# Pairwise softmax on VectorE, and b2 added by DMA, in a fused attention and MLP kernel on one Trainium2 core

## The chip, the cores and the metric

The kernel runs on one core of a Trainium2 chip. The metric is device time in microseconds (us); lower is better. A profile's span, from its first instruction to its last, is some 1.8 us shorter than the run's time.

PE is TensorE (PEld its weight loads), DVE is VectorE, ACT is ScalarE, POOL is GpSimd, and SP is the engine whose queue issues nearly all the DMAs. A "q" behind a name (SPq, POOLq) means the engine's instruction queue.

## The reference

```python
h  = x + attention(layernorm(x), wqkv) @ wo     # 32 heads of 18, window of 8 positions, 2 apart
h2 = h + gelu(layernorm(layernorm(h)) @ w1 + b1) @ w2 + b2
# x: 1 x 2048 x 576, w1: 576 x 4608, w2: 4608 x 576, all bf16
```

Each query attends to eight keys: its own position and those 2, 4, ... 14 before it, with softmax over the eight.

## The kernel before

The 2048 rows are 16 tiles of 128 rows, worked in eight pairs. After a prologue (LN1 and the QKV products) the program for PE is, for each pair: the first MLP matmul of this pair (four "visits" of two or three PSUM banks each, result `pm`), the output projection of the next pair (`pw`), and the second MLP matmul of this pair (result `po`, two tiles). The other engines work ahead: for the next pair, `h` and LN2; for the pair after that, attention. The last two pairs use a Strassen-like scheme with seven products, whose sums of w2 blocks VectorE prepares earlier.

The softmax of one tile, by VectorE with one exp on ScalarE:

```python
def att_qk_b(j, skip=0):
    att_qk_add(j, ((0, 0, 9), (0, 0, 4), (0, 0, 2), (0, 0, 1))[skip:])
    logits = sb.tile([P, W, H], F32, tag="logits", name="logits", bufs=2)
    nc.vector.tensor_tensor(out=logits[:], in0=prod[:, :, 0:H], in1=prod[:, :, 8 * H:9 * H], op=ALU.add)
    # ... causal mask of row 0
    nc.vector.tensor_reduce(out=mx[:], in_=logits[:].rearrange("p w h -> p h w"), axis=AX.X, op=ALU.max)
    nc.vector.tensor_tensor(out=logits[:], in0=logits[:], in1=mx[:].unsqueeze(1).to_broadcast([P, W, H]),
                            op=ALU.subtract)
```

A tile's keys and values are used by its own attention and then replaced by a copy shifted by one row, which comes back from DRAM. That is the "halo": `halo(j, 1)` fetches keys and `halo(j, 2)` values, both through the SP queue. And a transposed tile (LN2's output as `hnT`, attention's output o as `oT`) is written to DRAM (`td`) and read back by a transposing DMA, also through the SP queue, which stands still until the write has landed:

```python
def dma_transpose(dst, src):
    td = dma_out(src)
    nc.sync.dma_start_transpose(out=dst, in_=td[:])
```

LN2 of a pair ended with b2 added on VectorE, so that `x_all` holds the residual for the output addition:

```python
def add_b2(j):
    nc.vector.tensor_tensor(out=x_all[:, j, :], in0=h_of.pop(j)[:], in1=b2_bc[:], op=ALU.add)
```

The kernel keeps a PSUM bank's first half visit and second half visit on PE apart: a no-op on GpSimd, the "marker", waits for the first, and PE waits for it before the second.

## Time and profile before

| | before |
|---|---|
| median | 371.94 us (371.36, 371.82, 372.05, and one run of 542.28) |
| span, granted clock | 369.8 us, 0.998 |
| PE, VectorE, ScalarE busy | 98%, 81%, 65% |

The first three runs of the kernel before, without the 371.82, have the median of 372.05 us that the prediction starts from.

The page's table of engines of the kernel before (busy us, share of the span, instructions):

```profile
PE 363.2 (98%) x4944; PEld 299.4 (81%) x4944; DVE 299.3 (81%) x452; ACT 239.1 (65%) x519; POOL 25.2 (7%) x35
```

The waits of PE in the kernel before (who waited for whom: us in total, times, longest):

```profile
PE busy L661 <- DVE prod L654: 1.5, 1, 1.5
PE pm L209 <- ACT hT L490: 0.5, 1, 0.5
...
```

The chain of waits of the kernel before, one pair of it (start, us, what):

```profile
108.72 17.79 PE pm L209 x324
126.52 2.21 PE pw L209 x36
128.72 17.75 PE po L505 x144
146.47 17.79 PE pm L209 x324
```

The chain is followed back from the last instruction. From the second pair on it is PE and nothing else until the last addition, 37.75 us for each pair. VectorE's 81% is therefore an average over work that PE hides.

### The profile page before, as it was taken

The numbers are of one execution on the slowest core, as the hardware profiler recorded it, in microseconds if no ns is written. First come the engines' busy times: TensorE is split into PE (matmuls) and PEld (weight loads), VectorE is DVE, ScalarE is ACT, GpSimd is POOL, SyncE is SP. The second block draws the span as 40 slices with busy tenths as digits, with TensorE's granted clock in tenths as the row PEclk, the third lists the DMA queues.
The fourth block names the chain that finished last, engine by engine and source line by source line (L and its number), as shares of the span: only waits on it lengthen the run. The fifth ranks groups of instructions, "written<-read, shape, count | busy, mean of one in ns | idle before, by whom it ended". The sixth has DMA issues, their size and how long they took to land.

```text
span 369.8 us, 11478 instructions
## 1 busy us (share of the span) xinstructions
PE 363.2 (98%) x4944; PEld 299.4 (81%) x4944; DVE 299.3 (81%) x452; ACT 239.1 (65%) x519; POOL 25.2 (7%) x35
## 2 busy tenths in 40 slices
PE   7999999999999999999999999999999999999996
PEld 4789877888788877887788778877887788778874
DVE  6899999999999798979897989889898986532332
ACT  2688756797738793679366936693669456735630
POOL 2322004000300010001000100000000000000000
PEclk9999999999999999999999999999999999999999
DMA  8979798956445104710431043104320411030000
GB/s 242 318 198 282 190 204 235 331 178 76 141 107 166 35 15 111 275 35 2 110 97 37 2 106 102 37 2 105 86 52 3 105 52 39 0 89 18 4 0 32
DMA packets 57265, 38.96 MB, mean 105 GB/s; under 512 B 31344, under 2 KB 55536, under 8 KB 57216
## 3 DMA queue, kind: packets, MB, share of 16 engines
q1 hardware_dynamic: 57056, 38.18, 38.6%
q8 instruction: 38, 0.62, 0.7%
q10 hardware_dynamic: 160, 0.07, 0.1%
q14 instruction: 11, 0.09, 0.1%
HBM read 19.92 MB, written 12.42 MB: 87 GB/s over the span
## 4 chain that ended last, share of the span: by engine, by line
PE 84%; DVE 11%; ACT 2%; POOL 1%; issue 1%; POOLq 0%; DVEq 0%
PE pm L209 37%; PE po L505 29%; PE po L576 8%; PE pw L209 5%; PE pq L209 4%; DVE ln_stats L145 2%; DVE prod L323 2%; DVE prod L362 1%; DVE prod L317 1%; PE busy L661 1%; DVE prod L366 1%; POOL ln_rstd L156 1%; ACT hT L490 1%; DVE ln_mv L146 1%; ACT L463 0%
## 5 line engine op out<-in xcount | busy, mean ns | idle before, releaser
L209 PE MATMUL pm<-hnT,w_sb 64*128 64x256 bf16 x2304 | 143.0, 269 | 0.5 <-ACT hT L490 0.5
L490 ACT ACTIVATE hT<-pm,b_sb 128x256 bf16<-128x256 f32 (+1 forms) x288 | 108.5, 498 | 48.4 <-PE pm L209 48.4
L209 PEld LDWEIGHTS <-w_sb 64*128 64x128 bf16 x2304 | 112.5, 94 | 15.0 <-issue 2.3
L505 PEld LDWEIGHTS <-hT 128*128 128x128 bf16 x864 | 84.0, 98 | 22.6 <-issue 1.7
L505 PE MATMUL po<-w2a_sb,hT 128*128 128x288 bf16 x672 | 84.5, 286 | 0.0
L209 PE MATMUL pq<-wq_sb,xnT 64*128 64x288 bf16 x768 | 54.0, 283 | 0.4 <-ACT xnT L255 0.2
L209 PEld LDWEIGHTS <-xnT 64*128 64x128 bf16 x864 | 44.1, 94 | 9.1 <-issue 0.4
L323 DVE TENSOR_TENSOR prod<-prod 128x2304 bf16<-128x2304 bf16 (+1 forms) x64 | 44.2, 691 | 2.1
L362 DVE TENSOR_TENSOR prod<-kv_ring,a 128x4608 bf16<-128x4608 bf16 x16 | 40.9, 2558 | 0.6
L317 DVE TENSOR_TENSOR prod<-kv_ring,q_all 128x4608 bf16<-128x4608 bf16 x16 | 40.8, 2552 | 0.2
L209 PE MATMUL pm<-hnT,w1h_sb 64*128 64x256 bf16 x288 | 39.4, 269 | 0.0
L366 DVE TENSOR_TENSOR prod<-prod 128x2304 bf16<-128x2304 bf16 (+1 forms) x32 | 33.9, 1058 | 1.1
L345 ACT ACTIVATE logits<-logits 128x256 f32<-128x256 f32 x16 | 6.7, 417 | 38.1 <-DVE logits L334 38.1
L423 POOL TENSOR_TENSOR ln_rstd<-ln_var,mhalf 128x1 f32<-128x1 f32 x14 | 11.3, 810 | 249.8 <-ACT ln_var L422 249.6
L505 PE MATMUL po<-w2b_sb,hT 128*128 128x288 bf16 x192 | 25.5, 286 | 0.0
L294 ACT CAST kv_ring<-pq 128x576 bf16<-128x576 f32 x32 | 19.4, 641 | 8.4 <-PE pq L209 8.4
L407 DVE TENSOR_TENSOR h<-pw,x_all 128x576 f32<-128x576 f32 x16 | 11.4, 751 | 14.0 <-PE pw L209 14.0
L209 PE MATMUL pw<-wo_sb,oT 64*128 64x288 bf16 x256 | 19.5, 283 | 0.2
L463 ACT ACT_TABLE_LOAD x14 | 18.0, 1283 | 0.2
L552 DVE TENSOR_TENSOR prod<-hT 128x512 f16<-128x512 f16 (+1 forms) x8 | 3.6, 455 | 17.6 <-ACT hT L490 17.6
L209 PEld LDWEIGHTS <-oT 64*128 64x128 bf16 x288 | 13.9, 94 | 4.3 <-POOLq L219 0.8
L345 ACT ACT_TABLE_LOAD x13 | 16.7, 1283 | 0.2
(98 smaller groups left out, 340.4 us busy)
## 6 DMA issues: line engine op xcount, KB each, us to landing
w_sb<-in_B_w_dram SPq DMA_DIRECT2D x6, 768.0 KB, 6.0
kv_ring<-kv_dram SPq DMA_DIRECT2D x28, 144.0 KB, 2.8
w2a_sb<-in_B_w_dram SPq DMA_DIRECT2D x4, 1008.0 KB, 6.5
kv_dram<-kv_ring SPq DMA_DIRECT2D x13, 288.0 KB, 3.5
out_dram<-o_sb SPq DMA_DIRECT2D x15, 144.0 KB, 2.9
td<-q_all SPq DMA_DIRECT2D x14, 144.0 KB, 2.4
td<-hn SPq DMA_DIRECT2D x14, 144.0 KB, 1.8
wq_sb<-in_A_wqkv_dram SPq DMA_DIRECT2D x3, 576.0 KB, 5.9
```

The source lines that it names most:

```text
L209: last = nc.tensor.matmul(duo["g"][r ^ swap][i], lhsT=lhsT, rhs=rhs, start=(swap == 0 and i == 0 and kt == 0), stop=(swap == 1 and kt == K ...
L294: pace[0] = nc.scalar.copy(out=dst.rearrange("p (d g h) -> p g d h", g=2, h=H // 2), in_=ps[:, :, 0:HALF].rearrange("p g (h d) -> p g d h" ...
L317: nc.vector.tensor_tensor(out=prod[:], in0=k_ring[j % 2], in1=q_all[:, j, :].unsqueeze(1) .to_broadcast([P, W, D]), op=ALU.mult)
L323: nc.vector.tensor_tensor(out=prod[:, :, o * H:o * H + n], in0=prod[:, :, a * H:a * H + n], in1=prod[:, :, c * H:c * H + n], op=ALU.add)
L345: nc.scalar.activation(out=logits[:], in_=logits[:], func=ACT.Exp, scale=SCALE)
L362: nc.vector.tensor_tensor(out=prod[:].rearrange("p w (d h) -> p w d h", h=H), in0=v_ring[j % 2].rearrange("p w (d h) -> p w d h", h=H), in ...
L366: nc.vector.tensor_tensor(out=prod[:, 0:n, :], in0=prod[:, 0:n, :], in1=prod[:, n:2 * n, :], op=ALU.add)
L407: nc.vector.tensor_tensor(out=h[:].rearrange("p (g c) -> p g c", g=2), in0=pw[:, :, 0:HALF], in1=x_all[:, j, :].rearrange("p (g c) -> p g ...
L463: nc.scalar.activation(out=warm[:], in_=mhalf[:], func=ACT.Gelu_apprx_tanh)
L490: pace[0] = nc.scalar.activation(out=hT[us[i // GF]][:, GF * r + i % GF, 0:N], in_=ps[:, r, i * N:(i + 1) * N], func=ACT.Gelu_apprx_tanh, ...
L505: nc.tensor.matmul(banks[half], lhsT=hT[f // (2 * GF)][:, f % (2 * GF), i * P:(i + 1) * P], rhs=w2_rows(f)[:, half * HALF:(half + 1) * HAL ...
L576: nc.tensor.matmul(bank, lhsT=l, rhs=r, start=(start and m == 0), stop=(m == NM - 1), skip_group_check=True)
```

## The change

Its intent is to relieve VectorE. From the fifth pair on, both tiles of a pair share one max, subtract, exp, sum, reciprocal and multiply; the fourth pair shares them too, in another order. Each addition of b2 becomes two DMAs: b2 is copied into `x_all` through the SP queue, and `h` is added to it by an accumulating DMA from GpSimd, made to wait for both LN2 transposes of the pair. The first and the last pair keep VectorE. One o of the third pair is sent and read back in two steps. The core of the diff:

```diff
+    def att_max(js):
+        n, sl = len(js), sides(js)
+        nc.vector.tensor_reduce(out=peak[:, sl], in_=logits[:, sl].rearrange("p i w h -> p i h w"), axis=AX.X, op=ALU.max)
+        nc.vector.tensor_tensor(out=logits[:, sl], in0=logits[:, sl],
+                                in1=peak[:, sl].unsqueeze(2).to_broadcast([P, n, W, H]), op=ALU.subtract)
+    def att_qk_pair(e, f):
+        for i, j in enumerate((e, f)):
+            att_qk_a(j)
+            halo(j, 1)
+            att_qk_b(j, i)
+        att_max([e, f])
+    def put_b2(j):
+        nc.sync.dma_start(out=x_all[:, j, :], in_=b2_bc[:])
+    def accumulate_h(j):
+        ins = nc.gpsimd.dma_start(out=x_all[:, j, :], in_=h_of.pop(j)[:], accum_op=ALU.add).ins
+        tc.add_manual_dep(ins, read[0].name, sync_dep, reason="behind the transposes of LN2")
 ... 
             elif c is not None:                       # all pairs but the first and last
-                m1[0].append(c_(pv_t, d))
-                if e is not None:
-                    m1[3] = m1.get(3, []) + [c_(att_qk, e)] + [c_(w2_sums, *m) for m in T_SUMS.get(k, ())]
-                    ia[0] = [c_(exps, e)]
-                ia[0] = ia.get(0, []) + [c_(wo_visit, (c, "B"), (d, "C")), c_(ln2_pair, c, d, e)]
 ... (k == 1, in which the fourth pair's attention is worked out, has lines of its own)
+                elif e is not None:
+                    m1[1] = [c_(att_qk_pair, e, f)]
+                    m1[3] = [c_(w2_sums, *m) for m in T_SUMS.get(k, ())]
+                    ia[0] = [c_(exps, e, f), wo, c_(ln2_pair, c, d, (e, f)), c_(dma_tr_o, e)]
                 ib[0] = [c_(finish_out, g[0])]
                 if e is not None:
-                    ia[2] = [c_(pv_sum, e), c_(dma_tr_o, e)]
-                    ib[2] = [c_(att_qk, f)] + ([c_(halos, 7)] if k == 1 else [])
-                    ib[32] = [c_(exps, f)]
+                    ib[2] = [c_(pv_sum, f), c_(dma_tr_o, f)]
```

`m1[n]` is work queued before visit n of the first MLP matmul, `ia[n]` and `ib[n]` work queued at step n of the second one's two tiles. So, from the fifth pair on, the attention of a pair's two tiles, which was spread over the whole period, is now back to back: both logit passes, then the w2 sums, and only then `h` (inside `ln2_pair`).

More of the change, by code (lines that the diff above doesn't have):

```diff
@@ L82 @@
     prod = wpool.tile([P, W, D], BF16, name="prod")
+    logits = wpool.tile([P, 2, W, H], F32, name="logits")
+    probs = wpool.tile([P, 2, W, H], BF16, name="probs")
+    peak = wpool.tile([P, 2, H], F32, name="peak")
+    den = wpool.tile([P, 2, H], F32, name="den")
     qp_cm = tc.tile_pool(name="qkvw", bufs=1)
@@ L140, in ln_stats @@
         n = len(srcs)
-        stats = sb.tile([P, n, 2, nc.vector.BN_STATS_DIM], F32, tag=f"{tag}_stats", name=f"{tag}_stats", bufs=bufs)
-        mv = sb.tile([P, n, nc.vector.BN_AGGR_DIM], F32, tag=f"{tag}_mv", name=f"{tag}_mv", bufs=bufs)
+        pool = qp if tag.startswith("ln1") else sb
+        stats = pool.tile([P, n, 2, nc.vector.BN_STATS_DIM], F32, tag=f"{tag}_stats", name=f"{tag}_stats", bufs=bufs)
+        mv = pool.tile([P, n, nc.vector.BN_AGGR_DIM], F32, tag=f"{tag}_mv", name=f"{tag}_mv", bufs=bufs)
         for i, src in enumerate(srcs):
@@ L306, in tr_b1, with sides @@
         nc.scalar.copy(out=b1_sb[:], in_=pt)
-    e_of = {}
+    side = {}
+    def sides(js):
+        i = side[js[0]]
+        return slice(i, i + len(js))
     def halo(j, t):
@@ L324, in att_qk_add, with att_qk_b, att_qk_rest, att_qk @@
                                     in1=prod[:, :, c * H:c * H + n], op=ALU.add)
-    def att_qk_b(j, skip=0):
+    def att_qk_b(j, i, skip=0):
+        side[j] = i
         att_qk_add(j, ((0, 0, 9), (0, 0, 4), (0, 0, 2), (0, 0, 1))[skip:])
-        logits = sb.tile([P, W, H], F32, tag="logits", name="logits", bufs=2)
-        nc.vector.tensor_tensor(out=logits[:], in0=prod[:, :, 0:H], in1=prod[:, :, 8 * H:9 * H], op=ALU.add)
+        nc.vector.tensor_tensor(out=logits[:, i], in0=prod[:, :, 0:H], in1=prod[:, :, 8 * H:9 * H], op=ALU.add)
         if j // 2 + 1 < W:
-            nc.vector.memset(logits[0:1, j // 2 + 1:W, :], -1e9)
-        mx = sb.tile([P, H], F32, tag="mx", name="mx")
-        nc.vector.tensor_reduce(out=mx[:], in_=logits[:].rearrange("p w h -> p h w"), axis=AX.X, op=ALU.max)
-        nc.vector.tensor_tensor(out=logits[:], in0=logits[:], in1=mx[:].unsqueeze(1).to_broadcast([P, W, H]),
-                                op=ALU.subtract)
-        e_of[j] = logits
-    def att_qk(j):
+            nc.vector.memset(logits[0:1, i, j // 2 + 1:W, :], -1e9)
+    def att_max(js):
[3 more added lines that the diff above has]
+                                in1=peak[:, sl].unsqueeze(2).to_broadcast([P, n, W, H]), op=ALU.subtract)
+    def att_qk_rest(j, i, skip=0):
+        att_qk_b(j, i, skip)
+        att_max([j])
+    def att_qk(j, i):
         att_qk_a(j)
         halo(j, 1)
-        att_qk_b(j)
-    def att_exp(j):
-        logits = e_of[j]
-        nc.scalar.activation(out=logits[:], in_=logits[:], func=ACT.Exp, scale=SCALE)
+        att_qk_rest(j, i)
+    def att_qk_pair(e, f):
[4 more added lines that the diff above has]
+        att_max([e, f])
+    def att_exp(*js):
+        sl = sides(js)
+        nc.scalar.activation(out=logits[:, sl], in_=logits[:, sl], func=ACT.Exp, scale=SCALE)
     def att_pv(j):
@@ L349, in att_pv, with att_den @@
         att_pv_sum(j)
-    def att_den(j):
-        e = e_of.pop(j)
-        den = sb.tile([P, H], F32, tag="den", name="den")
-        nc.vector.tensor_reduce(out=den[:], in_=e[:].rearrange("p w h -> p h w"), axis=AX.X, op=ALU.add)
-        nc.vector.reciprocal(out=den[:], in_=den[:])
-        a = sb.tile([P, W, H], BF16, tag="a", name="a")
-        nc.vector.tensor_tensor(out=a[:], in0=e[:], in1=den[:].unsqueeze(1).to_broadcast([P, W, H]), op=ALU.mult)
-        e_of[j] = a
+    def att_den(*js):
+        n, sl = len(js), sides(js)
+        nc.vector.tensor_reduce(out=den[:, sl], in_=logits[:, sl].rearrange("p i w h -> p i h w"), axis=AX.X, op=ALU.add)
+        nc.vector.reciprocal(out=den[:, sl], in_=den[:, sl])
+        nc.vector.tensor_tensor(out=probs[:, sl], in0=logits[:, sl],
+                                in1=den[:, sl].unsqueeze(2).to_broadcast([P, n, W, H]), op=ALU.mult)
     def att_pv_sum(j):
-        a = e_of.pop(j)
+        a = probs[:, side.pop(j)]
         nc.vector.tensor_tensor(out=prod[:].rearrange("p w (d h) -> p w d h", h=H),
                                 in0=v_ring[j % 2].rearrange("p w (d h) -> p w d h", h=H),
-                                in1=a[:].unsqueeze(2).to_broadcast([P, W, Dh, H]), op=ALU.mult)
+                                in1=a.unsqueeze(2).to_broadcast([P, W, Dh, H]), op=ALU.mult)
         for n in (4, 2):
@@ L386, in dma_tr_o, with send_o, read_o @@
         dma_transpose(new_oT(j)[:], q_all[:, j, :])
-    pw_of = {}
+    def send_o(j):
+        o_sent[j] = dma_out(q_all[:, j, :])
+    def read_o(j):
+        nc.sync.dma_start_transpose(out=new_oT(j)[:], in_=o_sent.pop(j)[:])
+    pw_of, o_sent = {}, {}
     def wo_duo(j, tag):
@@ L430, in ln2_send @@
         hn[j] = dma_out(y[:])
+    read = [None]
     def ln2_in(j):
-        nc.sync.dma_start_transpose(out=hnT_slot(j), in_=hn.pop(j)[:])
+        read[0] = nc.sync.dma_start_transpose(out=hnT_slot(j), in_=hn.pop(j)[:]).ins
     def add_b2(j):
         nc.vector.tensor_tensor(out=x_all[:, j, :], in0=h_of.pop(j)[:], in1=b2_bc[:], op=ALU.add)
+    def put_b2(j):
[3 more added lines that the diff above has]
+        tc.add_manual_dep(ins, read[0].name, sync_dep, reason="behind the transposes of LN2")
     def ln2_rstd(j):
@@ L722, in pv_t, with ln2_pair @@
             dma_tr_o(j)
-        def ln2_pair(c, d, e, b2=True):
+        def ln2_pair(c, d, js=()):
+            last = c == GROUPS[-1][0]
             for j in (c, d):
@@ L728, in ln2_pair @@
             for j in (c, d):
-                if b2:
-                    add_b2(j)
+                (add_b2 if last else put_b2)(j)
+            if js:
+                att_den(*js)
+                att_pv_sum(js[0])
+            for j in (c, d):
                 ln2_send(j)
+            if len(js) == 2:
+                halo(js[0], 2)
             for j in (c, d):
                 ln2_in(j)
-            if e is not None:
-                att_den(e)
+            if not last:
+                for j in (c, d):
+                    accumulate_h(j)
+            if len(js) == 1:
+                halo(js[0], 2)
         loads = {v: [c_(load_w1, c)] for c, v in enumerate((3, 4, 9, 14, 16, 18))}
@@ L747 @@
             6: [c_(ln1_rstd, 10), c_(ln1_act, 8, 2), c_(halo, A[0], 1)],
-            7: [c_(att_qk_b, A[0]), c_(ln1_bias, 10), c_(ln1_act, 8, 3), c_(in_x, 0), c_(out_x, 1)],
-            8: [c_(att_qk_a, A[1]), c_(att_qk_b, A[1]), c_(ln1_act, 9, 0)],
+            7: [c_(att_qk_rest, A[0], 0), c_(ln1_bias, 10), c_(ln1_act, 8, 3), c_(in_x, 0), c_(out_x, 1)],
+            8: [c_(att_qk_a, A[1]), c_(att_qk_rest, A[1], 1), c_(ln1_act, 9, 0)],
             9: [c_(halo, A[1], 1), c_(in_x, 1)],
@@ L760 @@
             19: [c_(ln2, A[1])],
-            20: [c_(ln2_rstd, A[1]), c_(add_b2, A[1]), c_(ln2_bias, A[1]), c_(att_qk_b, A[2], 1)],
+            20: [c_(ln2_rstd, A[1]), c_(add_b2, A[1]), c_(ln2_bias, A[1]), c_(att_qk_rest, A[2], 0, 1)],
         }
@@ L817, in halos, with exps @@
                 store_halo(pending_halo.pop(0))
-        def exps(j):
-            att_exp(j)
+        def exps(*js):
+            att_exp(*js)
             gelu_table()
@@ L836 @@
             if k == 0:
-                m1[0] += [c_(halos, 1), c_(att_qk_a, d), c_(att_qk_b, d), c_(halo, d, 1)]
+                m1[0] += [c_(halos, 1), c_(att_qk_a, d), c_(att_qk_rest, d, 1), c_(halo, d, 1)]
                 mid[0] = [c_(exps, d)]
-                m1[1] = [c_(pv_t, c), c_(pv_t, d), c_(load_w2, 4), c_(att_qk, e)]
+                m1[1] = [c_(pv_t, c), c_(pv_t, d), c_(load_w2, 4), c_(att_qk, e, 0)]
                 ia[0] = [c_(wo_visit, (c, "B"))]
-                ia[12] = [c_(exps, e), c_(wo_visit, (d, "A")), c_(ln2_pair, c, d, e, False), c_(pv_sum, e), c_(dma_tr_o, e), c_(halos, 2)]
+                ia[12] = [c_(exps, e), c_(wo_visit, (d, "A")), c_(ln2_pair, c, d, (e,)), c_(halos, 2), c_(send_o, e)]
@@ L842 @@
                 ib[0] = [c_(finish_out, g[0])]
-                ib[4] = [c_(att_qk, f)]
+                ib[4] = [c_(att_qk, f, 1)]
+                ib[8] = [c_(read_o, e)]
                 ib[32] = [c_(exps, f)]
             elif c is not None:
-                m1[0].append(c_(pv_t, d))
+                wo = c_(wo_visit, (c, "B"), (d, "C"))
                 if k == 1:
-                    m1[0] += [c_(add_b2, j) for j in g]
-                if e is not None:
-                    m1[3] = m1.get(3, []) + [c_(att_qk, e)] + [c_(w2_sums, *m) for m in T_SUMS.get(k, ())]
-                    ia[0] = [c_(exps, e)]
@@ L852 @@
-                ia[0] = ia.get(0, []) + [c_(wo_visit, (c, "B"), (d, "C")), c_(ln2_pair, c, d, e)]
+                    m1[0].append(c_(pv_t, d))
+                    m1[1] = [c_(att_qk_a, e), c_(halo, e, 1), c_(att_qk_b, e, 0), c_(halos, 7)]
+                    m1[3] = [c_(att_qk_a, f), c_(halo, f, 1), c_(att_qk_add, f, ((0, 0, 9), (0, 0, 4)))]
+                    ia[0] = [wo, c_(ln2_pair, c, d), c_(att_qk_b, f, 1, 2), c_(att_max, (e, f)), c_(exps, e, f), c_(att_den, e, f)]
+                    ia[2] = [c_(pv_sum, e), c_(dma_tr_o, e)]
+                elif e is not None:
+                    m1[1] = [c_(att_qk_pair, e, f)]
+                    m1[3] = [c_(w2_sums, *m) for m in T_SUMS.get(k, ())]
+                    ia[0] = [c_(exps, e, f), wo, c_(ln2_pair, c, d, (e, f)), c_(dma_tr_o, e)]
+                else:
+                    ia[0] = [wo, c_(ln2_pair, c, d)]
```

## The prediction

> **What bounds the kernel now.** TensorE. The engine table gives PE 363.2 us of a 369.8 us span (98%), VectorE 299.3 (81%), ScalarE 239.1 (65%), at a granted clock of 0.998. The chain of waits runs through VectorE and GpSimd only up to 54.9 us; from 78.95 us to 366.35 us it is PE alone: per pair of tiles 17.79 us (first MLP matmul), 2.21 us (projection), 17.75 us (second), the same in each of five pairs. The table of waits lists 0.5 us of PE waiting for a GELU at 78.9 us and nothing over 0.3 us after the start. So VectorE work is already hidden behind PE, and the listing of instructions shows PE's order unchanged, row for row.
>
> **What the change removes, adds and moves.** VectorE loses, per pair: two b2 additions (0.67 us each by their spacing) and fixed costs of the paired max, subtract, sum, reciprocal and multiply (estimate 0.3 to 0.6 us, from 0.59, 0.43, 0.35 us for single ones). That is roughly 2 us of 37.75, about 10 us in all. ScalarE loses one exp and two table loads (1.28 us each) per later pair. Added: twelve 144 KB copies of b2 on the SP queue and twelve accumulating DMAs issued by GpSimd, each pair's behind its LN2 transposes. None of what is removed is on the critical path, so the gain I count is 0.
>
> **Where it could cost.** Two boundaries have no slack.
> 1. First to second pair. The last LN2 transpose is issued at 105.4 us and takes 2.9 us to land, so 108.35; PE starts on it at 108.66. GpSimd will then issue two accumulating DMAs, and its next job is the marker that PE needs about 2.2 us into the visit (two half visits of 1.1 us), at 110.9. The Trainium skill, "DMA: Bandwidth & Descriptors", section "SWDGE vs HWDGE vs iDMA", says that accumulate and cast go through GpSimd and that it writes the descriptors by software; the trace before has no such DMA, so the cost is unseen. At an estimated 1 us each the markers are just in time; at 2 us each PE stalls by some 1.6 us. GpSimd's power took 1.5 us here beside a busy VectorE against 0.55 elsewhere, so slow issue is possible. In later pairs the transposes land 2 to 3.5 us before PE needs them, so issue is hidden.
> 2. Second to third pair. The exp of that pair waits behind LN2 on ScalarE, VectorE idles some 4 us (133 to 137), and both weighted sums follow. I work out the last output addition at about 151.5 us; PE wants that PSUM bank at 151.55. Estimate 0 to 0.5 us of stall.
>
> In later pairs the value halo goes ahead of the transposes (0.5 us of issue) and the double exp adds 0.2 us, inside their slack.
>
> **Prediction.** 372.3 us against 372.05; range 371.0 to 374.3. Faster by over 2%: 0.01; within 2%: 0.95; slower by over 2%: 0.04.
>
> **What would show it right or wrong.** VectorE's busy time down by some 10 us (to about 289) and ScalarE's by 12 to 20, with PE's busy time unchanged and the three steady lengths still 17.79, 2.21 and 17.75 us: VectorE savings are worth nothing. New PE waits, if any, are near 110 us (on GpSimd's queue) and near 151 us (on the output addition), 2 us in sum at most. Transposes still landing before each first matmul confirm the rest.
>
> **What would make it wrong.** GpSimd taking over 3 us per accumulating DMA, which would stall PE in six pairs, by 2% or more in the worst case; transposes slowed by copies beside them beyond their 2 us of slack; or the slow outlier seen once before (542 us) becoming common.

## The result, and the profile after

| | before | changed |
|---|---|---|
| median | 371.94 us | 372.54 us (372.49, 372.75, 372.59, 371.52) |
| ratio | | 1.0018, 95% interval 1.0002 to 1.0035 |
| span, granted clock | 369.8 us, 0.998 | 370.7 us, 1.0 |

A ratio is the mean time of one kernel's runs over that of the other's of the same rounds, so it is not quite the ratio of the medians. Executions over 1.5% slower than the fastest of the same kernel are left out of the means.

The table of engines of the changed kernel:

```profile
PE 363.6 (98%) x4944; PEld 299.1 (81%) x4944; DVE 286.9 (77%) x415; ACT 225.5 (61%) x499; POOL 41.1 (11%) x47
```

VectorE lost 12.4 us of work and ScalarE 13.6 us. The time did not fall; it rose by about 0.2%. PE's own lengths are the old ones, as the chain of waits of the changed kernel shows for the third pair (start, us, what):

```profile
146.91 17.79 PE pm L214 x324
164.70 2.21 PE pw L214 x36
166.90 17.75 PE po L539 x144
```

The waits of PE in the changed kernel; the one for `hnT` is new:

```profile
PE busy L695 <- DVE prod L688: 1.5, 1, 1.5
PE pm L214 <- ACT hT L524: 0.5, 1, 0.5
...
PE pm L214 <- DMA hnT<-td: 0.5, 1, 0.5
...
```

**A cleaner clock.** The prologue has the same order on PE in both kernels, yet the MLP began at times from 69.23 to 70.51 us over twelve profiles, without relation to the change. So I also give the "MLP length", from the start of the first `pm` matmul to the start of the last pair's second matmul, which leaves that jitter out. The timeline of PE gives it, here of the kernel before (start, us, instruction):

```profile
69.36 0.60 PE L209 MATMUL pm<-hnT,w_sb 64*128 64x256 bf16 x8
...
350.70 1.52 PE L576 MATMUL po<-w2a_sb,hT 128*128 128x288 bf16 x11
```

The same view of the changed kernel:

```profile
69.80 0.60 PE L214 MATMUL pm<-hnT,w_sb 64*128 64x256 bf16 x8
...
351.66 1.52 PE L610 MATMUL po<-w2a_sb,hT 128*128 128x288 bf16 x11
```

The lengths are 281.34 and 281.86 us. So of the 0.9 us between the two spans, 0.44 us is a later start of the MLP (prologue jitter) and 0.5 us was lost in the MLP, where the new wait is 0.45 us.

**Where the 0.45 us comes from.** It is the LN2 transpose of the seventh pair, in the sixth pair's period. The chain of waits of the changed kernel leaves PE at 270 us and returns at 298 us (start, us, what):

```profile
260.14 10.17 PE pm L214 x184
270.31 0.25 SPq L196
...
271.22 2.22 DMA kv_ring<-kv_dram
...
273.47 2.57 DVE prod L326
...
284.74 1.33 DVE h L432 x2
...
295.39 2.90 DMA hnT<-td
...
298.33 17.86 PE pm L214 x324
```

Read it forwards. The SP queue is at the transposing read of an o (L196). It had waited there for the write of that o to land, then issues an output store (L668), and only then the key halo, which lands at 273.45 us. VectorE needs the halo for the second tile's logit pass. Behind that stand the rest of the softmax and eight w2 sums, so `h` starts at 284.66 us. LN2, its writes, and the two transposes follow; the last one lands at 298.29 us. PE had been free since 297.88 us. In the kernel before, VectorE was early at this place and waited for PE; its timeline there:

```profile
279.25 1.42 DVE L407 TENSOR_TENSOR h<-pw,x_all 128x576 f32<-128x576 f32 x2 [1.59 <-PE pw L209]
```

The timeline of the SP queue of the changed kernel at that place (start, us, instruction):

```profile
263.33 0.97 SPq L191 DMA_DIRECT2D td<-q_all  x1
268.39 2.16 SPq L196 DMA_TRANSPOSE oT<-td  x1
270.60 0.58 SPq L668 DMA_DIRECT2D out_dram<-o_sb  x1
271.22 0.43 SPq L323 DMA_DIRECT2D kv_ring<-kv_dram  x1
...
292.98 0.43 SPq L191 DMA_DIRECT2D td<-hn  x1
293.51 0.40 SPq L323 DMA_DIRECT2D kv_ring<-kv_dram  x1
294.08 2.53 SPq L460 DMA_TRANSPOSE hnT<-td  x2
```

The timeline of VectorE of the changed kernel there (in brackets the idle time before an instruction and who ended it):

```profile
273.47 2.56 DVE L326 TENSOR_TENSOR prod<-kv_ring,q_all 128x4608 bf16<-128x4608 bf16 x1 [4.25 <-DMA kv_ring<-kv_dram]
```

VectorE stands idle 4.25 us. Two smaller terms follow after `h`. The lower lines of the SP queue show the value halo (293.51) between LN2's last write and the transposes: 0.57 us from its issue to theirs. And the second tile's power on GpSimd, a step of LN2, now begins inside the long multiplication of VectorE's weighted sum; in the kernel before it fell between two of VectorE's additions. The timeline of GpSimd at this pair, in the kernel before:

```profile
287.45 0.55 POOL L423 TENSOR_TENSOR ln_rstd<-ln_var,mhalf 128x1 f32<-128x1 f32 x1 [0.97 <-ACT ln_var L422]
```

and in the changed kernel:

```profile
289.51 1.83 POOL L448 TENSOR_TENSOR ln_rstd<-ln_var,mhalf 128x1 f32<-128x1 f32 x1 [1.33 <-ACT ln_var L447]
```

The Trainium skill, "SBUF — State Buffer", section "SBUF: two separate sides", says that VectorE operations with two SBUF inputs and GpSimd operations that read SBUF lock a port pair against each other for a whole instruction. For GpSimd the trace agrees: the power started while VectorE multiplied two SBUF tiles (288.37 to 290.93 us) and ended 0.41 us after it, having taken 1.83 us instead of 0.55. All three terms together made PE late by 0.45 us; by these numbers each of them alone is larger than that, so without any one of them PE would likely not have waited; the runs below test only what makes `h` late.

Over the run the waits of VectorE in the changed kernel hold two lines that before has none of:

```profile
DVE prod L326 <- DMA kv_ring<-kv_dram: 13.1, 4, 4.3
DVE prod L381 <- DMA kv_ring<-kv_dram: 7.4, 4, 2.9
```

That is 20.5 us of waiting for halos, more than the 12.4 us of work saved. The waits for key halos, which come before `h`, ate the slack of LN2. The table gives, in us, how long after PE began the projection `h` started, and how long before PE began the next pair the first LN2 transpose was issued (worked out from the chains and timelines; both transposes need 4.2 us: the second is issued 1.3 us after the first and lands 2.9 us later).

| pair whose second matmul runs | 2 | 3 | 4 | 5 | 6 |
|---|---|---|---|---|---|
| `h` after the projection's begin, before | 1.75 | 1.75 | 1.76 | 1.76 | 1.76 |
| the same, changed | 1.86 | 3.99 | 5.55 | 5.85 | 6.73 |
| transpose ahead of PE, before | 7.00 | 6.99 | 6.21 | 7.01 | 6.96 |
| the same, changed | 10.17 | 5.15 | 4.97 | 4.66 | 4.25, with PE waiting |

### The profile page after: what moved, and what is told of

The parts are those of the page before. It is cut to its first block, busy times and chain, and to the rows that moved or that the text cites. A ratio compares the mean times of both kernels' runs of the same rounds, so it can differ in the third digit from the quotient of the medians.

```text
span 370.7 us, 11474 instructions
## 1 busy us (share of the span) xinstructions
PE 363.6 (98%) x4944; PEld 299.1 (81%) x4944; DVE 286.9 (77%) x415; ACT 225.5 (61%) x499; POOL 41.1 (11%) x47
## 4 chain that ended last, share of the span: by engine, by line
PE 80%; DVE 14%; ACT 2%; DMA 1%; issue 1%; SPq 1%; POOL 0%; DVEq 0%; POOLq 0%
PE pm L214 35%; PE po L539 24%; PE po L610 8%; PE pq L214 6%; PE pw L214 4%; DVE prod L332 2%; DVE prod L381 2%; DVE prod L326 2%; DVE prod L385 2%; PE busy L695 1%; ACT hT L524 1%; DVE x_all L573 1%; DMA hnT<-td 1%; PE xt_pt L181 1%; DVE peak L344 1%
## 5 line engine op out<-in xcount | busy, mean ns | idle before, releaser
L326 DVE TENSOR_TENSOR prod<-kv_ring,q_all 128x4608 bf16<-128x4608 bf16 x16 | 40.8, 2549 | 13.2 <-DMA kv_ring<-kv_dram 13.1
L381 DVE TENSOR_TENSOR prod<-kv_ring,probs 128x4608 bf16<-128x4608 bf16 x16 | 40.9, 2558 | 7.8 <-DMA kv_ring<-kv_dram 7.4
L448 POOL TENSOR_TENSOR ln_rstd<-ln_var,mhalf 128x1 f32<-128x1 f32 x14 | 16.1, 1151 | 190.3 <-ACT ln_var L447 190.3
L161 POOL TENSOR_TENSOR ln_rstd<-ln_veps,mhalf 128x1 f32<-128x1 f32 (+2 forms) x13 | 13.3, 1026 | 49.3 <-DVE ln_veps L155 40.3
L469 POOL DMA_DIRECT2D x_all<-h x12 | 10.9, 1060 | 44.4 <-DMA td<-q_all 30.2
L214 PEld LDWEIGHTS <-w1h_sb 64*128 64x128 bf16 x288 | 14.1, 94 | 1.6
L150 DVE BATCH_NORM_STATS2 ln_stats<-x_all 128x6 f32<-128x288 bf16 x32 | 12.8, 443 | 2.4 <-DMA x_all<-in_A_x_dram 2.4
```

The costliest lines, as they stand in the source:

```text
L150: nc.vector.bn_stats(out=stats[:, i, c, :], in_=src[:, c * HALF:(c + 1) * HALF])
L161: nc.gpsimd.tensor_tensor(out=rstd[:], in0=veps[:], in1=mhalf[:].to_broadcast([P, n]), op=ALU.pow)
L214: last = nc.tensor.matmul(duo["g"][r ^ swap][i], lhsT=lhsT, rhs=rhs, start=(swap == 0 and i == 0 and kt == 0), stop=(swap == 1 and kt == K ...
L326: nc.vector.tensor_tensor(out=prod[:], in0=k_ring[j % 2], in1=q_all[:, j, :].unsqueeze(1) .to_broadcast([P, W, D]), op=ALU.mult)
L381: nc.vector.tensor_tensor(out=prod[:].rearrange("p w (d h) -> p w d h", h=H), in0=v_ring[j % 2].rearrange("p w (d h) -> p w d h", h=H), in ...
L448: nc.gpsimd.tensor_tensor(out=rstd[:], in0=var[:], in1=mhalf[:], op=ALU.pow)
```

## The experiments

Theory, as first formed from the two traces: PE is the limit, so VectorE's savings are worth nothing, and the small loss is VectorE delivering `h` late because of the new order. On why the halo is late there were two versions: A, the accumulating DMAs crowd the DMA engines; B, the order of the SP queue alone. The rival to all of it: the loss is chance, or comes from the accumulating DMAs directly. Ten kernels ran, the first four on one chip, the next four on a second, the last two on a third; each set shares its runs of the kernel before (nine each, medians 371.75, 371.74 and 371.69 us). Diffs are shortened.

| run | median us | ratio to before, 95% interval | MLP length us |
|---|---|---|---|
| again_after | 372.37 | 1.0026 (1.0012 to 1.0039) | 281.49 |
| vector_b2 | 374.03 | 1.0063 (1.0050 to 1.0077) | 283.39 |
| split_f | 371.62 | 0.9999 (0.9986 to 1.0013) | 281.33 |
| sums_late | 371.57 | 1.0001 (0.9987 to 1.0015) | 281.60 |
| before_no_b2 | 371.71 | 0.9998 (0.9985 to 1.0012) | 281.32 |
| before_dma_b2 | 371.92 | 1.0007 (0.9995 to 1.0020) | 281.33 |
| accum_halves | 372.84 | 1.0030 (1.0006 to 1.0054) | 283.60 |
| before_late_exp | 371.78 | 1.0002 (0.9989 to 1.0014) | 281.26 |
| accum_early | 376.21 | 1.0125 (1.0105 to 1.0146) | 286.10 |
| three_orders | 371.50 | 0.9993 (0.9979 to 1.0007) | 281.34 |

### again_after: the changed kernel again

> The changed kernel again, unchanged, in five rounds, to set the size of the difference. In its first profile the chain is 0.44 us later than before's when the MLP starts (69.97 against 69.53 us; prologue, where the instruction order is the same), and PE loses 0.45 us to a late LN2 transpose at 298 us. If the first is jitter of the start and the second is a property of the change, the ratio is about 1.001 (0.5 us of 372) and the second profile again has one PE wait of 0.2 to 0.8 us on the transpose of the seventh pair near 298 us, while the start of the MLP may fall anywhere from 69.4 to 70.1 us. Rival: the loss is a matter of chance and the wait is not there again.

The loss is there again: ratio 1.0026, on another chip. The profile fell on the fastest of its five runs (371.71 us), and there the first transpose was issued 4.28 us before PE took it; PE began the pair at 297.56 us, 0.1 us late, less than the 0.2 to 0.8 us expected. The waits for halos are there again (11.3 us for keys, 9.1 for values). So the lateness of `h` belongs to the change, while the miss at this place is small and differs from run to run. What the slower, unprofiled runs (up to 373.02 us) lost, and where, no profile shows.

### before_no_b2: VectorE work taken from the kernel before

```diff
     def add_b2(j):
-        nc.vector.tensor_tensor(out=x_all[:, j, :], in0=h_of.pop(j)[:], in1=b2_bc[:], op=ALU.add)
+        h_of.pop(j)
```

> The kernel before with the sixteen VectorE additions of b2 left out altogether (the result is wrong on purpose: the residual is x and b2 is missing). VectorE loses some 10.7 us of work and nothing is added anywhere. My theory (PE is the limit, VectorE work of this kind is hidden): VectorE busy near 288 us, time unchanged, ratio 0.999 to 1.001, except that the two additions in the prologue (0.7 us each, on the chain's VectorE part before 55 us or just after it) may give up to 0.5 us. Rival (VectorE is close to limiting): 2 us or more are won.

The result is wrong, as meant. VectorE's busy time fell from 299.3 to 289.2 us, and the ratio is 0.9998. This settles the main point: 10 us less of VectorE work, with nothing added, is worth nothing here.

### before_dma_b2: the b2 part alone

```diff
-                if b2:
-                    add_b2(j)
+                (add_b2 if last else put_b2)(j)
 ...
+            if not last:
+                for j in (c, d):
+                    accumulate_h(j)
```

> The kernel before with only the b2 part of the change: copies of b2 on the SP queue and accumulating DMAs behind the transposes, softmax by single tiles as before. If the loss of the change comes from the pairwise order of VectorE, this one equals before: no PE wait over 0.3 us at any pair's start, h starts 1.7 to 1.9 us after the projection's begin as in before, ratio 0.999 to 1.001. Rival (the accumulating DMAs themselves cost): transposes land late, PE waits at one or more pairs, or PE waits for GpSimd's markers, ratio over 1.002.

MLP length 281.33 us, no new PE wait in the MLP, and VectorE waits 2.0 us for halos in all instead of 20.5. In the old order the accumulating DMAs cost nothing that the profile shows. So the loss belongs to the new order, or to the two together.

### vector_b2: pairwise softmax with b2 on VectorE

```diff
-                (add_b2 if last else put_b2)(j)
+                add_b2(j)
 ...
-            if not last:
-                for j in (c, d):
-                    accumulate_h(j)
```

> The changed kernel with b2 added by VectorE in every pair; no copies of b2, no accumulating DMA. Theory A (the accumulating DMAs crowd the DMA engines, so that the projection input of the pair's second tile lands late, the SP queue stands still behind it, the key halo goes out late and VectorE waits): the VectorE waits for the halo (13.1 us for keys, 7.4 us for values) fall to under half, h starts under 3 us after PE begins the projection in pairs 3 to 6, the PE wait at 298 us is gone, time 0.3 to 0.6 us shorter than the changed kernel, equal to before. Rival B (order alone: the two logit passes now stand back to back with one halo between them, and the SP queue holds that halo behind the transpose of the second tile's o, whatever the DMA traffic): the waits stay over 10 us in sum, VectorE has 0.67 us times 12 more work, h is later still and the PE wait is as long or longer, by up to 1.3 us.

Neither version held. The waits for halos fell from 20.5 to 14.1 us: by a third, not by half as A wanted, and to over 10 us as B wanted. `h` starts 4.88 and 5.16 us after the projection's begin in the last two columns of the table (5.85 and 6.73 in the changed kernel, 1.76 before), where A wanted under 3. So traffic adds to the lateness and order makes most of it. What traffic does can be seen at the write of o that the SP queue stood still for. The view of the tile `td` (the copy of o in DRAM) in the changed kernel, at 262.8 to 263.6 us, has

```profile
DMA to landing us min/median/max: 4.9/5.1/5.2
```

beside the two accumulating DMAs (issued at 260.15 and 260.74 us, landed by 267.22), and that of vector_b2, which has none, at 264.4 to 266.0 us:

```profile
DMA to landing us min/median/max: 1.8/2.3/2.8
```

The wait at the seventh pair, which B wanted longer, is not there. That does not speak for A, since PE was already 1.7 us late by then, which gave the transposes room. This kernel is the slower one for another reason. The waits of PE in vector_b2:

```profile
PE pm L214 <- DVE o_sb L666: 1.7, 1, 1.7
```

The timeline of VectorE in vector_b2 at that place:

```profile
152.42 0.75 DVE L666 TENSOR_TENSOR o_sb<-po,x_all 128x576 bf16<-128x576 f32 x1
```

and in the changed kernel:

```profile
151.04 0.75 DVE L666 TENSOR_TENSOR o_sb<-po,x_all 128x576 bf16<-128x576 f32 x1
```

This is the third pair's start, the second boundary that the prediction named. The output addition frees the PSUM bank that PE takes second in its second visit. In the kernel before it ended at 147.26 us and PE wanted the bank at 151.43; in the changed kernel it ends at 151.79 us and PE wants the bank at 151.87, so of 4.2 us only 0.08 are left; here it ends at 153.17 us, and PE waits 1.73 us. The additions of b2 of the second and of the third pair, 1.3 us of VectorE for each pair, stand ahead of it (one pair's worth is taken up by VectorE's idle time before an exp, which falls from 4.2 to 2.8 us), and a key halo comes 0.44 us late. So the accumulating DMAs have a purpose after all: the pairwise order makes this boundary tight, and taking b2 from VectorE is what just keeps it.

### split_f: each o of a later pair sent, and read back behind the key halo

```diff
-    def att_qk_pair(e, f):
+    def att_qk_pair(e, f, waiting):
         for i, j in enumerate((e, f)):
             att_qk_a(j)
             halo(j, 1)
+            if i == 0:
+                read_o(waiting)
             att_qk_b(j, i)
 ...
-                    m1[1] = [c_(att_qk_pair, e, f)]
+                    m1[1] = [c_(att_qk_pair, e, f, d)]
 ...
+                    m1[0] = m1[0] + [c_(read_o, d)]       # the pair that has no further attention
 ...
-                    ib[2] = [c_(pv_sum, f), c_(dma_tr_o, f)]
+                    ib[2] = [c_(pv_sum, f), c_(send_o, f)]
```

> The changed kernel with o of the second tile of each pair from the fourth on sent at once and read back only after the next pair's first key halo has been issued, so that the SP queue no longer holds the halo behind the transpose. Theory B (order of the SP queue): VectorE's wait for key halos falls from 13.1 to under 5 us, h starts 2 to 4 us earlier in pairs 3 to 6, the PE wait at 298 us is gone; time 0.3 to 0.6 us shorter than the changed kernel. Theory A (traffic): the halo itself still lands late, waits stay over 9 us. In both, nothing beyond 0.6 us is won, since PE has no other waits.

This kernel moves only a DMA issue (it starts with the second o of the fourth pair): the write of o is sent where it was, and the transposing read stands later in the queue, so that the queue need not stand still between them. The key halo of the sixth pair's period is now issued at 265.00 us, ahead of the read. The SP queue of split_f:

```profile
262.62 0.99 SPq L191 DMA_DIRECT2D td<-q_all  x1
263.71 1.25 SPq L670 DMA_DIRECT2D out_dram<-o_sb  x1
265.00 0.43 SPq L323 DMA_DIRECT2D kv_ring<-kv_dram  x1
267.64 1.21 SPq L413 DMA_TRANSPOSE oT<-td  x1
```

and VectorE's logit pass that had waited 4.25 us:

```profile
268.21 2.56 DVE L326 TENSOR_TENSOR prod<-kv_ring,q_all 128x4608 bf16<-128x4608 bf16 x1 [0.19 <-DMA kv_ring<-kv_dram]
```

The key halo waits fell from 13.1 to 0.2 us, `h` starts 1.88, 3.53, 1.81, 1.82 and 1.81 us after the projection's begin (1.86, 3.99, 5.55, 5.85 and 6.73 in the changed kernel), and the wait of PE is gone: MLP length 281.33 us, as before the change. The waits for value halos rose, from 7.4 to 11.6 us, but they come after `h`. The accumulating DMAs are all still there, and the write of o still takes 4.9 us to land at this place. So changing the order of the SP queue alone is enough to take the wait away: order carries the lateness that reached PE, and traffic, which makes the write slow that the queue stands still for, is a smaller part of it (version B, with something of A).

### sums_late: the w2 sums behind h

```diff
-                    m1[3] = [c_(w2_sums, *m) for m in T_SUMS.get(k, ())]
 ...
-                ib[0] = [c_(finish_out, g[0])]
+                ib[0] = [c_(finish_out, g[0])] + [c_(w2_sums, *m) for m in T_SUMS.get(k, ())]
```

> The changed kernel with VectorE's sums of w2 blocks moved from before the LN2 input h to after the first output addition of the pair, where VectorE waits for the value halo anyway. The halo waits stay, but h no longer stands behind 2.7 to 3.2 us of sums: h starts within 2.5 us of the projection's begin in pairs 3 to 6, the transposes land over 1 us before PE needs them, the PE wait at 298 us is gone, time 0.3 to 0.6 us shorter than the changed kernel, that is equal to before. If the PE wait comes from elsewhere (traffic beside the transposes themselves), it stays.

The key halo waits stay (13.2 us), but VectorE comes to `h` sooner: 2.21, 1.76, 2.40, 1.84 and 2.13 us after the projection's begin, and PE's wait near 298 us is gone. This is a second and independent remedy: either a shorter wait or less work between the wait and `h` is enough. The MLP length is 281.60 us all the same, 0.26 us over that of before. PE waited 0.10 us at 151.56 us for the output addition, which had ended at 151.50 us, and the third pair took 0.27 us longer than the others. That is the second boundary again. Up to there this kernel is the changed kernel, instruction for instruction; what differed is a key halo that came 0.21 us late at 123.98 us. So the changed kernel's 0.08 us can be kept or missed from run to run.

### accum_halves: each accumulating DMA in two

```diff
-        ins = nc.gpsimd.dma_start(out=x_all[:, j, :], in_=h_of.pop(j)[:], accum_op=ALU.add).ins
-        tc.add_manual_dep(ins, read[0].name, sync_dep, reason="behind the transposes of LN2")
+        h = h_of.pop(j)
+        for cols in (slice(0, HALF), slice(HALF, D)):
+            ins = nc.gpsimd.dma_start(out=x_all[:, j, cols], in_=h[:, cols], accum_op=ALU.add).ins
+            tc.add_manual_dep(ins, read[0].name, sync_dep, reason="behind the transposes of LN2")
```

> The changed kernel with each accumulating DMA cut into two halves of 288 columns, so that GpSimd issues four for a pair instead of two. In the changed kernel the two took 1.8 to 2.0 us of GpSimd and ended 0.25 to 0.6 us before PE wanted the next marker, in five of six pairs. If issue costs about 0.9 us whatever the size, GpSimd ends 1.8 us later and PE waits 1.2 to 1.9 us for the marker in those five pairs: 5 to 8 us in all, time 377 to 380 us. If the cost goes by size, nothing changes (372.5 us). This tests the step of the prediction that put the danger in GpSimd's issue time.

This tests the first boundary that the prediction named: GpSimd, busy issuing, comes late to its marker, and PE waits. The timeline of GpSimd in accum_halves:

```profile
109.41 3.77 POOL L471 DMA_DIRECT2D x_all<-h  x4 [7.39 <-DVE logits L338]
```

and the marker's line in the same stretch:

```profile
L224 POOLq EVENT_SEMAPHORE  x2: 17/17/17, 110.8 to 111.4; - x2
```

Four issues took 3.77 us where two took 1.97 us in the changed kernel, so a half costs GpSimd as much as a whole. Yet the markers ran at 110.8 and 111.4 us, in the middle of that time, and PE has no wait on GpSimd here. The expected stall did not come, and the step "its next job is the marker" is refuted: in these traces an issue that is still being worked on does not hold the marker up. (The changed kernel's own trace shows it already: a marker ran at 110.41 us, while the second issue lasted from 109.87 to 111.11 us.)

What slowed this kernel (runs of 374.18, 373.27, 371.63 and 372.41 us) is another wait. The waits of PE in accum_halves, its profile being that of the 374.18 us run:

```profile
PE pm L214 <- DVE o_sb L668: 2.1, 1, 2.1
```

It is the start of the third pair once more. A halo that VectorE needs there came 2.19 us late at 126.50 us, and everything behind it moved. Its timed runs scatter by 2.5 us, which fits a boundary that is kept or missed by how the DMAs of a run fall, but only one of them has a profile.

### before_late_exp: a late GELU of the kernel before

Both kernels have a PE wait of 0.5 us for a GELU near 79 us, because ScalarE takes the exp of a tile first. This run, of the kernel before, moves that exp from inside the first visit to behind it (and changes the order of PSUM banks of the first pair to suit).

```diff
-                mid[0] = [c_(exps, d)]
-                m1[1] = [c_(pv_t, c), c_(pv_t, d), c_(load_w2, 4), c_(att_qk, e)]
+                m1[1] = [c_(exps, d), c_(pv_t, c), c_(pv_t, d), c_(load_w2, 4), c_(att_qk, e)]
 ...
-            mlp1(g, "pair", m1, mid)
+            mlp1(g, "first" if k == 0 else "pair", m1, mid)   # "first": its last visit uses banks D, C, A
```

> The kernel before with one PE wait taken away, the 0.47 us for a GELU at 78.9 us: the exp of the first pair's lookahead tile moves from between the two GELU sets of the first visit to behind both, and the last visit of that pair takes its first two PSUM banks in the other order, so that the delayed banks are wanted last. If PE is the limit, the whole 0.47 us comes off: the MLP's second pair starts 0.4 to 0.5 us earlier relative to the MLP's start, ratio 0.998 to 0.9995. If the wait only moves to another bank, the ratio is 0.9995 to 1.001.

The GELU wait is gone from the waits of PE, and a new one stands in its place:

```profile
PE pw L209 <- DMA oT<-td: 0.6, 1, 0.6
```

PE came to the second tile's projection sooner and wanted its o at 92.55 us; it landed at 93.12. That o is no later than it was: VectorE made it 17.93 us after the MLP's start here and 17.91 us in the kernel before, where it landed just in time (at 92.31 us, for PE at 92.41). Ratio 1.0002, MLP length 281.26 us against 281.34: the wait was moved, not removed.

### accum_early: the accumulating DMAs not held back

```diff
         ins = nc.gpsimd.dma_start(out=x_all[:, j, :], in_=h_of.pop(j)[:], accum_op=ALU.add).ins
-        tc.add_manual_dep(ins, read[0].name, sync_dep, reason="behind the transposes of LN2")
 ...                                       # moved up: right behind put_b2, ahead of LN2's writes
+            if not last:
+                for j in (c, d):
+                    accumulate_h(j)
 ...                                       # and taken away behind the transposes
-            if not last:
-                for j in (c, d):
-                    accumulate_h(j)
```

> The changed kernel with the accumulating DMAs no longer behind the LN2 transposes: GpSimd issues them as soon as the copy of b2 has landed and the two powers are done, about 3 to 5 us earlier, so that they run beside the writes of the LN2 output and the transposes. If they crowd the DMA engines (one takes 5.4 us to land), the LN2 transposes land 0.5 to 2 us later than in the changed kernel, the PE waits at one or more pairs, time 0.5 to 4 us over the changed kernel's 372.4. If traffic of this size does not matter, the transposes still land 2.9 us after their issue and the time is that of the changed kernel or a little better, because the reads of o are no longer crowded.

This is the slowest of all: 376.21 us, ratio 1.0125, MLP length 286.10 us. The result is correct. The waits of PE in accum_early:

```profile
PE pm L214 <- DMA hnT<-td: 3.7, 4, 1.9
...
PE pm L214 <- DVE o_sb L665: 0.4, 1, 0.4
```

The timeline of the SP queue of accum_early at the second pair's LN2:

```profile
103.47 0.67 SPq L191 DMA_DIRECT2D td<-hn  x1
104.30 4.67 SPq L460 DMA_TRANSPOSE hnT<-td  x2
```

and of the changed kernel:

```profile
103.70 0.43 SPq L191 DMA_DIRECT2D td<-hn  x1
104.30 2.65 SPq L460 DMA_TRANSPOSE hnT<-td  x2
```

In accum_early GpSimd issues both DMAs at 101.79 to 103.75 us, beside these writes. The second tile's last write takes 4.2 us to land instead of 2.0, so the second transpose is issued at 107.8 instead of 105.7 us. The transposes themselves are little slower (3.8 and 3.0 us to land at this pair, where the changed kernel's take 2.8). So the wait "behind both LN2 transposes" is a good part of the change, worth some 4 us, and what it protects is chiefly the write that the transpose waits for. The Trainium skill, "DMA: Bandwidth & Descriptors", section "Rules for kernel authors", says that a transpose next to ordinary DMAs needs nothing. It says so of correct data, and with that this run agrees; of time it says nothing, and time is what was lost here.

### three_orders: the orders mended together

This run joins split_f and sums_late, and moves the fourth pair's second weighted sum, with the sending of its o, behind the last output addition, to give the second boundary room. (The expectation calls it the third pair's; by the kernel it is the fourth's.) The diff against the changed kernel, without the lines of split_f and sums_late that were shown:

```diff
                     m1[1] = [c_(att_qk_pair, e, f, d)]
+                    if k == 2:
+                        m1[0] += [c_(pv_sum, d), c_(send_o, d)]
 ...
-                if e is not None:
+                if e is not None and k > 1:
                     ib[2] = [c_(pv_sum, f), c_(send_o, f)]
```

> The changed kernel with three orders mended, no work removed: o of each second tile sent and read back in two steps, the w2 sums behind the first output addition, and the second weighted sum of the third pair behind the last output addition instead of in front of it. If the loss is only the late h and the late output addition that runs of this kind showed (PE waits of 0.45, 1.7 and 2.1 us), none of them is left: the PE waits are those of before, every pair's h starts within 2.3 us of the projection's begin, the output addition at the third pair's start ends 3 us or more before PE wants the bank, and the time is before's: 371.4 to 371.9 us, ratio 0.999 to 1.001, no run over 372.4. It cannot be faster than before, since PE's own work is the same.

The output addition now runs at 147.65 us, directly behind PE, and is no longer near its limit. VectorE waits for PE at four of the pairs' `h` again (15.0 us in all), for key halos 0.2 us. MLP length 281.34 us: that of before to the hundredth. Median 371.50 us, ratio 0.9993 (0.9979 to 1.0007). One expectation was missed: a run came at 372.69 us, and it is the profiled one; there PE waited 0.9 us for QKV weights in the prologue and the MLP began at 70.51 us, which the change does not touch.

So with every deadline kept, the pairwise kernel is as fast as the one before and no faster, since PE's own work is the same. No version that beats both by more than the noise was found.

## Why the prediction was right or wrong

1. **"None of what is removed is on the critical path, so the gain I count is 0."** Right, and shown: before_no_b2 takes 10 us from VectorE and gains nothing, and the changed kernel takes 12.4 us from it with PE's lengths still 17.79, 2.21 and 17.75 us. VectorE's saving was sized at 10 us and measured 12.4: the paired operations save more than the 0.3 to 0.6 us a pair that was estimated. ScalarE's 13.6 us lay within the 12 to 20.
2. **First boundary, GpSimd's issue ahead of the marker.** The size was right (1.97 us for two), the step was wrong. No PE wait came, and accum_halves shows that even 3.77 us of issuing gives none, because the marker does not wait for the issue.
3. **Second boundary, the output addition at about 151.5 us against a bank wanted at 151.55.** The place was right, and it is the most fragile one that the runs found: 0.08 us to spare in the changed kernel's profile, and PE waits of 0.10 us in sums_late, 0.4 in accum_early, 1.7 in vector_b2 and 2.1 in accum_halves. In the profile of the changed kernel itself nothing was lost there.
4. **"In later pairs ... inside their slack."** This step failed. I counted a halo's issue (0.5 us) and a double exp (0.2 us) and took the slack of 2 to 3.5 us from the old order. I did not follow VectorE's new order: both logit passes, a halo between them that stands behind an o's transpose in the SP queue, and the w2 sums, all ahead of `h`. That made `h` late by up to 5 us, and at the sixth pair's period the transposes came 0.45 us too late. split_f and sums_late each take the wait away, by two different edits.
5. **"Transposes still landing before each first matmul confirm the rest."** They did at six of seven pairs. The wait at the seventh is the only new one in the profile.
6. **The size.** The prediction was 0.25 us over the time before; the result is 0.6 us over it by medians. The term that was too small is point 4's, counted as 0 and measured as 0.45 us in the changed kernel's profile. It need not be the same in every run: the profile of again_after shows 0.1 us there. That the predicted time came so near is in part luck: its 0.25 us stood for stalls near 110 and 151 us, neither of which came in the changed kernel's profile, and what was lost was lost at a place that the prediction had called safe.
7. **The 542 us outlier** did not become common: it never came again.

Still open: how much of the halos' lateness is traffic and how much order in numbers (vector_b2 says a third, but it shifts all deadlines too); what the slower of the changed kernel's unprofiled runs lost (the boundary near 151 us, with its 0.08 us, is a candidate, not shown); and what the 542 us run was.

## What to carry to other kernels

Where one engine is the limit, as PE at 98% of the span was here, work that it hides on another engine is worth nothing when it is taken away, but moving it is not free of danger: write down for each hand-over when it is due and when it will be ready, in the new order, and go through every in-order queue on the way, for batching can turn saved work into waits that eat the slack. A write and the transposing read that waits for it are better issued apart, with the transfers that others need sooner between them. And hold heavy, undated traffic back until the short transfers with deadlines are through, as the wait behind the transposes does here.

## What the Trainium skill lacked or had wrong

- "DMA: Bandwidth & Descriptors", section "Anatomy of one DMA — SWDGE (gpsimd) path", gives 2.0 us plus the bytes over 436e3, an estimate of 2.3 us for 144 KB. The accumulating DMAs of the changed kernel took 5.4 us to land in the median (3.5 to 6.5), beside other traffic. The page has no figure for accumulating ones (these also turn float32 into bf16).
- "DMA: Bandwidth & Descriptors", section "Rules for kernel authors": its "needs nothing" for a transpose next to ordinary DMAs is a rule about the data; what such neighbours cost in time it does not say. In accum_early the write ahead of a transpose landed in 4.2 instead of 2.0 us, and the kernel took some 4 us longer.
- "SBUF — State Buffer", section "SBUF: two separate sides": the lock is said to hold for the whole instruction of whichever engine starts first. A GpSimd power that started during a VectorE product of two SBUF tiles did wait for it (1.83 us instead of 0.55). The reverse was not seen: the first tile's power of the same pair ran from 287.61 to 288.17 us, VectorE's product `probs` of two SBUF tiles began 0.03 us after it, and took 0.70 us, where two others of its shape with no power beside them took 0.69 us. (A profile's spans on GpSimd are rough.)
